# Attention with cached K and V: how K of the first units is transposed, and how the last 64 contraction rows of Q are multiplied

## The chip, the cores and the metric

The kernel runs on one core of a Trainium2 chip. The metric is the device time of one execution in microseconds (us). Before the change it is 1075.5 us, the median of three runs (1074.76 to 1076.54).

A core has TensorE (PE, matrix products into PSUM), VectorE (DVE), ScalarE (ACT), GpSimd (POOL) and SyncE (SP), which here issues every DMA. A matmul on PE has a weight load ahead of it, shown in the profile as a separate row, PEld.

## The reference, cut to what matters

Two independent problems A and B of the same shape are computed, and their outputs are joined along the last axis. Types are bf16.

```python
# B = 16, Sq = 144, D = 448, H = 16, Sk = 512, Dh = 256
q = (x @ wq).reshape(B, Sq, H, Dh).transpose(0, 2, 1, 3)
scores = einsum("bhqd,bhkd->bhqk", q, k_cache) * Dh ** -0.5
p = softmax(scores, axis=-1)
o = einsum("bhqk,bhkd->bhqd", p, v_cache)
out = o.transpose(0, 2, 1, 3).reshape(B, Sq, H * Dh) @ wo
```

## The kernel before, in words

**Units.** One batch and one head of one problem is a unit, so there are 512. Each needs Q (the product of x and 256 columns of wq), S (K times Q, scores with keys on the partitions), an exponential on ScalarE, PV (V times the exponentials), a sum over keys (a product with a matrix of ones), its reciprocal on ScalarE as exp(-ln), and a scaled evacuation into a ring of outputs on VectorE (line 1241). The output projection OP (line 1306) takes pieces of that ring in between.

**K transposed.** S needs K with the head dimension on the partitions. For units 48 and up the DMA transposes K as it loads it, 16 units (4 MB) at a time, into one of two halves of `kt_sb` (`t_load_k`, line 966). For the first 48 units (`P0`) K is loaded as it stands into slots of `v_sb` (`t_load_n`, line 987), and PE transposes it by 128x128 blocks against an identity (`t_tr`, line 1006): four blocks into a bank shared with S, which VectorE evacuates, and four into a bank shared with Q, which ScalarE evacuates (both line 1014).

**Q.** The contraction is over 448 rows, three chunks of 128 and a last one of 64. `q_pair` says how many units one Q makes: one (80 times, all of the first 48 units among them), or two units of the same head in neighbouring batches, with both batches' queries as one moving operand of 288 columns (216 times). The last 64 rows of wq stand in a tile of their own, `wr_sb`: rows for the first 128 output columns on partitions 0 to 63, and those for the other 128 on partitions 64 to 127. Two-unit Q runs the last chunk as two matmuls of 64 rows each, on the two halves of the array (line 1099). One-unit Q runs it as one full matmul of 288 columns (line 1087), against a moving tile `xz_sb` that holds x twice, each copy zero on the half that isn't its own. x is loaded transposed with rows 320 to 447 as its fourth chunk, so its last 64 rows are on partitions 64 to 127 only. VectorE copies them to partitions 0 to 63 (line 1049, for two-unit Q) or into `xz_sb` (lines 1055 and 1058), one step of the schedule ahead of the Q that reads them (`t_q_rest`).

**Order.** A Python loop over steps writes each engine's program; a recording layer (`_Sched`) adds the semaphore waits that reads and writes of the same tile or bank need. Every engine executes its program in order. One step has, on PE: half of a transposition for the unit four ahead, Q for a unit three or four ahead, S two or three ahead, the other half of the transposition, PV and the sum of the current unit, then OP pieces. SyncE's order is a list: a start table, loads by due time, and a table for the change from problem A to B. There `q0` to `q3` load B's wq in groups of four heads, each as three DMAs (lines 926, 930, 931) on one semaphore, between V loads and the K loads `k16`, `k17` and `k18`. A load that waits for a buffer holds up all that stand behind it.

**Start.** The first DMAs are K of the first two units, wq of the first four heads, then x. GpSimd meanwhile writes ones and selects the identity from them (line 917). It lies in a slot of `qt_sb` that is used for Q later.

Of the kernel before, what the change touches and what calls it, by code (L numbers as in the profile page):

```python
# [5 lines left out]
BF16 = mybir.dt.bfloat16  # L6
F32 = mybir.dt.float32
# [745 lines left out]
def bass_concat_heads__mha_block_cached__gqa_block_cached__near_ridge_kernel(  # L753
# [67 lines left out]
    with contextlib.ExitStack() as es:  # L821
# [5 lines left out]
        def ps(name, shape, dt):  # L827
            return mem.enter_context(nc.psum_tensor(name, shape, dt))

        wq_sb = sb("wq_sb", [128, 3, H * DH], BF16)  # L830
        wr_sb = sb("wr_sb", [128, H * 128], BF16)
        xz_sb = sb("xz_sb", [128, 2, 2, SQ], BF16)
        wo_sb = sb("wo_sb", [128, NWO, D], BF16)
        ring = sb("ring", [128, NWO, RC], BF16)
        kt_sb = sb("kt_sb", [128, 8, KR * 128], BF16)
# [16 lines left out]
        s_ps = [ps("s_ps%d" % i, [128, 512], F32) for i in range(3)]  # L852
        ot_ps = [ps("ot_ps%d" % i, [128, 512], F32) for i in range(2)]
        op_ps = ps("op_ps", [128, 512], F32)
        tr_ps = (s_ps[2][:, :].bitcast(BF16), qp_ps[:, 1, :].bitcast(BF16))
        ident = qt_sb[:, NQT - 1, 0, 0:128]
        id_key = (("qt", NQT - 1), -1)

        S = _Sched()
# [37 lines left out]
        def t_init():  # L897
            def e0(v):
                return v.memset(stat[:, 0:2], 0.0)
            S.add(DVE, e0, writes=[("scr", 0)], name="statz")  # L900

            def e1(a):
                a.preload_act_table_set("natural_log_exp_and_others")
                return a.activation(stat[0:1, 1:2], stat[0:1, 0:1], AF.Exp)
            S.add(ACT, e1, reads=[("scr", 0)], writes=[("scr1", 0)], name="actwarm")

            def e2(v):
                v.memset(xz_sb[64:128, :, 0, :], 0.0)
                return v.memset(xz_sb[0:64, :, 1, :], 0.0)
            S.add(DVE, e2, writes=[("xzz", 0)], name="xzz")  # L910

            def e4(g):
                return g.memset(ones[:], 1.0)
            S.add(POOL, e4, writes=[("ones", 0)], name="ones")

            def e5(g):
                return g.affine_select(ident, ones[:], pattern=[[1, 128]], compare_op=ALU.is_equal,
                                       fill=0.0, base=0, channel_multiplier=-1)
            S.add(POOL, e5, reads=[("ones", 0)], writes=[id_key], name="ident")

        def t_load_wq(pr, hg):
            cols = slice(hg * 4 * DH, (hg + 1) * 4 * DH)
            w = wqs[pr]

            def e(q):
                q.dma_start(wq_sb[:, 0:3, cols], w[0:384, cols].rearrange("(c p) n -> p c n", p=128)).then_inc(
                    sems["wq%d" % hg], 16)
                last = w[384:448, cols].rearrange("k (h e m) -> k h e m", e=2, m=128)
                dst = wr_sb[:, hg * 512:(hg + 1) * 512].rearrange("p (h m) -> p h m", m=128)
                q.dma_start(dst[0:64], last[:, :, 0, :]).then_inc(sems["wq%d" % hg], 16)  # L930
                return q.dma_start(dst[64:128], last[:, :, 1, :]).then_inc(sems["wq%d" % hg], 16)
            S.add(SP, e, writes=[(("wq", hg), pr)], dma_sem="wq%d" % hg, n_dma=3, name="wq%d.%d" % (pr, hg))

        def t_load_wo(pr, wg):
            c0 = wg * WOG
# [46 lines left out]
        def t_load_n(G):  # L982
# [4 lines left out]
                return q.dma_start(v_sb[:, sl, :, :], src).then_inc(sems["v%d" % sl], 16)  # L987
            S.add(SP, e, writes=[(("v", sl), ("n", G))], dma_sem="v%d" % sl, name="n%d" % G)

        def t_tr(U, k):  # L990
            G, j = divmod(U, UV)
            sl = v_seq["n", G] % NV
            ko = U % KR * 128

            kt_key = ("kt", U // KW % (KR // KW))
            if k == 0 and U % KW == 0:
                S.res[kt_key] = _Res()
                S.res[kt_key].version = U // KW
            bank, eng = (("s2", DVE), ("qp1", ACT))[k]
            key = (("sp", 2), "qp1")[k]  # L1000

            def e(t):
                ins = None
                for c in range(4):
                    a = (4 * k + c) * 128
                    ins = t.transpose(tr_ps[k][:, c * 128:(c + 1) * 128], v_sb[:, sl, j, a:a + 128], ident)  # L1006
                return ins
            S.add(PE, e, reads=[(("v", sl), ("n", G)), id_key], writes=[(key, ("t", U))], banks=[bank],
                  name="TR%d.%d" % (U, k))

            def ev(g):
                dst = kt_sb[:, 4 * k:4 * k + 4, ko:ko + 128]
                src = tr_ps[k][:, 0:512].rearrange("p (c q) -> p c q", c=4)
                return g.activation(dst, src, AF.Copy) if eng == ACT else g.tensor_copy(dst, src)  # L1014
            S.add(eng, ev, reads=[(key, ("t", U))], writes=[(("ktn", U % KR), U)], banks=[bank],
                  name="etr%d.%d" % (U, k))
# [25 lines left out]
            for u, sl in zip(q_units(U), free):  # L1042
                q_slot[u] = q_live[u] = sl

        def t_xr(g, n):
            gx = g % NX
            if n == 2:
                def e(v):
                    return v.tensor_copy(xt_sb[0:64, 3, gx, :], xt_sb[64:128, 3, gx, :])  # L1049
                S.add(DVE, e, reads=[(("xt", gx), g)], writes=[(("xr", gx), g)], name="xr%d" % g)  # L1050
                return
            z = g % 2

            def e0(v):
                return v.tensor_copy(xz_sb[0:64, z, 0, :], xt_sb[64:128, 3, gx, :])

            def e1(v):
                return v.tensor_copy(xz_sb[64:128, z, 1, :], xt_sb[64:128, 3, gx, :])
            for k, e in ((0, e0), (1, e1)):
                S.add(DVE, e, reads=[(("xt", gx), g), ("xzz", 0)], writes=[(("xz", z), g)], name="xz%d.%d" % (g, k))  # L1060

        xr_made = set()

        def t_q_rest(U):
            pr = unit(U)[0]
            n = q_pair(U)
            for u in q_units(U):
                g = pr * Bn + (u - pr * NU) // H
                if (g, n) not in xr_made:
                    xr_made.add((g, n))  # L1070
                    t_xr(g, n)

        def t_q(U):
            pr, b, h = unit(U)
            n = q_pair(U)
            gs = [pr * Bn + (u - pr * NU) // H for u in q_units(U)]
            xo, xe = gs[0] % NX, gs[-1] % NX
            hg = h // 4
            z = gs[0] % 2
            rest = [(("xz", z), gs[0])] if n == 1 else [(("xr", g % NX), g) for g in gs]  # L1080

            def e(t):
                ins = None
                xs_ = slice(xo, xe + 1, max(xe - xo, 1))
                wr = wr_sb[:, h * 128:(h + 1) * 128]
                if n == 1:
                    t.matmul(qp_ps[:, 0, 0:2 * SQ], lhsT=wr, rhs=xz_sb[:, z, :, :], start=True, stop=False,  # L1087
                             skip_group_check=True)
                for kc in range(3):
                    for dc in range(2):  # L1090
                        c0 = h * DH + dc * 128
                        acc = qp_ps[:, dc, 0:2 * SQ] if n == 2 else qp_ps[:, 0, dc * SQ:(dc + 1) * SQ]
                        ins = t.matmul(acc, lhsT=wq_sb[:, kc, c0:c0 + 128], rhs=xt_sb[:, kc, xs_, :],  # L1093
                                       start=(n == 2 and kc == 0), stop=(n == 1 and kc == 2),
                                       skip_group_check=(n == 1))
                if n == 2:
                    for dc in range(2):
                        p = slice(64 * dc, 64 * dc + 64)
                        ins = t.matmul(qp_ps[:, dc, 0:2 * SQ], lhsT=wr[p], rhs=xt_sb[p, 3, xs_, :],  # L1099
                                       start=False, stop=True)  # L1100
                return ins
            S.add(PE, e, reads=[(("wq", hg), pr)] + [(("xt", g % NX), g) for g in gs] + rest,
                  writes=[(bk, ("q", U)) for bk in q_banks[:n]], banks=q_banks[:n], name="Q%d" % U)

        def t_evac_q(U):
# [13 lines left out]
        def t_s(U):  # L1119
# [6 lines left out]
            for k in range(2):  # L1126
                bank = k if U < P0 else (2 * U + k) % 3

                def e(t, k=k, bank=bank):
                    ins = None  # L1130
                    for c in (2 * k, 2 * k + 1):
                        for dc in range(2):
                            ins = t.matmul(s_ps[bank][:, (c % 2) * SQ:(c % 2 + 1) * SQ],  # L1133
                                           lhsT=kt_sb[:, 2 * c + dc, ko:ko + 128],
                                           rhs=qt_sb[:, qsl, dc, :], start=(dc == 0), stop=(dc == 1))
                    return ins
                S.add(PE, e, reads=[(("qt", qsl), U), (("kt", ksl), W)] + kn, writes=[(("sp", bank), 2 * U + k)],
# [285 lines left out]
        while True:  # L1423
# [12 lines left out]
            u = i + LT  # L1436
            if 0 <= u < P0:
                t_tr(u, 0)
            for u in of_step(lq, i + 1):
                if q_pair(u):  # L1440
                    t_q_rest(u)
            for u in of_step(lq, i):
                if q_pair(u):
                    t_q_rest(u)
                    t_q(u)
                    t_evac_q(u)
            for u in of_step(ls, i):
# [138 lines left out]
```

## Time and profile before

| | |
|---|---|
| median of three runs | 1075.5 us |
| the profiled execution | 1075.5 us |
| its span, first instruction to last | 1073.7 us |
| granted TensorE clock, mean | 0.998 |
| PE, ACT, DVE, POOL busy | 98%, 74%, 70%, 59% |
| moved by DMA | 294 MB, mean 274 GB/s |
| S (L1133), PV (L1189), OP (L1306), Q (L1093, L1099) on the chain | 24, 22, 18 and 21% of the span |
| transposes (L1006) | 384 |

Matmuls are pipelined and the profile models their ends, so what a matmul costs is read from the distance between starts, and not from its duration: 128x144 matmuls are given as 226 ns long and start every 62 or 63 ns. Idle time of an engine is put down to what ended last before it resumed. The chain of work that ended last is followed back from the last instruction, at each step to what released it.

### The profile page before, as it was taken

How to read it: one execution, taken by the hardware profiler on the slowest of the kernel's cores; microseconds unless marked ns; L12 is line 12 of the kernel's file. 1: busy time of each engine (PE TensorE's matmuls, PEld its weight loads, DVE VectorE, ACT ScalarE, POOL GpSimd, SP SyncE). 2: the span in 40 equal slices, each digit the busy share in tenths (PEclk: the TensorE clock that was granted, in tenths of full speed). 3: DMA queues.
4: the chain of work that ended last, by engine and by line, in shares of the span. 5: the costliest groups of instructions: out<-in, count | busy, mean ns of one | idle time of the engine just before them, and what ended most of it. 6: DMA issues, size and time to landing. Idle time of an engine off the chain costs nothing.

```text
span 1073.7 us, 32198 instructions
## 1 busy us (share of the span) xinstructions
PE 1050.2 (98%) x12296; PEld 833.4 (78%) x12296; DVE 752.0 (70%) x2083; ACT 794.3 (74%) x2365; POOL 630.9 (59%) x1030
## 2 busy tenths in 40 slices
PE   7999999999999999999989999999999999999998
PEld 6998777777777777777867777777777777777785
DVE  4776666767766677677868676667776667777775
ACT  5876667777777777778857677777777777778785
POOL 3554555656656566666745555566665555666663
PEclk9999999999999999999999999999999999999999
DMA  9999999999999999999999999999999989999950
GB/s 340 388 325 254 311 275 299 264 249 259 259 299 289 245 252 248 286 298 272 267 296 329 265 287 305 288 304 286 305 268 277 254 241 306 274 293 233 264 192 13
DMA packets 592771, 294.13 MB, mean 274 GB/s; under 512 B 505056, under 2 KB 517856, under 8 KB 592608
## 3 DMA queue, kind: packets, MB, share of 16 engines
q1 hardware_dynamic: 592608, 291.99, 107.1%
q8 instruction: 98, 1.61, 0.6%
q14 instruction: 65, 0.53, 0.2%
HBM read 161.48 MB, written 4.13 MB: 154 GB/s over the span
## 4 chain that ended last, share of the span: by engine, by line
PE 91%; ACT 3%; DMA 3%; DVE 2%; issue 1%; SPq 0%; ACTq 0%; DVEq 0%
PE s_ps L1133 24%; PE ot_ps L1189 22%; PE op_ps L1306 18%; PE qp_ps L1093 17%; PE qp_ps L1099 4%; DMA kt_sb<-in_B_k_cache_dram 2%; ACT rinv_sb L1226 2%; PE ot_ps L1205 2%; PE qp_ps L1087 1%; ACT pt_sb L1143 1%; PE s_ps L1006 1%; PE qp_ps L1006 1%; DVE ring L1241 1%; DMA wr_sb<-in_B_wq_dram 1%; PE qp_ps L1306 1%
## 5 line engine op out<-in xcount | busy, mean ns | idle before, releaser
L1153 POOL TENSOR_TENSOR pp_sb<-pt_sb 128x288 f32<-128x288 bf16 x512 | 379.8, 742 | 347.0 <-ACT pt_sb L1143 334.1
L1143 ACT ACTIVATE pt_sb<-s_ps 128x288 bf16<-128x288 f32 x1024 | 364.6, 408 | 203.3 <-PE s_ps L1133 196.1
L1241 DVE TENSOR_TENSOR ring<-ot_ps,rinv_sb 128x288 bf16<-128x288 f32 (+2 forms) x640 | 242.0, 395 | 156.8 <-ACT rinv_sb L1226 154.5
L1133 PE MATMUL s_ps<-qt_sb,kt_sb 128*128 128x144 bf16 x4096 | 343.5, 227 | 2.5 <-DVE ring L1241 1.0
L1189 PE MATMUL ot_ps<-pt_sb,v_sb 128*128 128x144 bf16 x4096 | 340.0, 226 | 0.0
L1133 PEld LDWEIGHTS s_ps<-qt_sb,kt_sb 128*128 128x128 bf16 x4096 | 271.0, 98 | 69.9 <-DVE qt_sb L1112 3.0
L1226 ACT ACTIVATE rinv_sb<-ln_sb 64x144 f32<-64x144 f32 x928 | 298.2, 321 | 24.2
L1306 PE MATMUL op_ps<-wo_sb,ring 128*128 128x448 bf16 x1120 | 284.5, 352 | 0.0
L1189 PEld LDWEIGHTS ot_ps<-pt_sb,v_sb 128*128 128x128 bf16 x4096 | 274.2, 98 | 0.5
L1158 POOL TENSOR_TENSOR p_sb<-pp_sb 128x144 f32<-128x144 f32 x464 | 226.9, 489 | 74.8 <-DVE ps_sb L1167 10.7
L1093 PE MATMUL qp_ps<-xt_sb,wq_sb 128*128 128x288 bf16 (+1 forms) x1776 | 239.1, 271 | 5.6 <-DMA wr_sb<-in_B_wq_dram 4.1
L1093 PEld LDWEIGHTS qp_ps<-xt_sb,wq_sb 128*128 128x128 bf16 x1776 | 161.9, 98 | 71.4 <-DVE xt_sb L1049 6.1
L1256 DVE TENSOR_REDUCE run_sb<-ot_ps 128x1 bf16<-128x144 f32 x560 | 146.6, 304 | 87.5 <-ACT ln_sb L1213 55.6
L1167 DVE TENSOR_TENSOR ps_sb<-p_sb 64x144 bf16<-64x144 f32 x464 | 160.1, 345 | 37.5 <-POOL p_sb L1158 23.5
L1113 DVE CAST qt_sb<-qp_ps 128x576 bf16<-128x576 f32 x216 | 162.2, 751 | 18.1 <-PE qp_ps L1099 14.3
L1306 PEld LDWEIGHTS op_ps<-wo_sb,ring 128*128 128x128 bf16 x1120 | 93.9, 98 | 21.2
L1213 ACT ACTIVATE ln_sb<-ot_ps 128x144 f32<-128x144 f32 x232 | 67.7, 292 | 32.1 <-PE ot_ps L1205 24.4
L1099 PE MATMUL qp_ps<-xt_sb,wr_sb 64*128 64x288 bf16 x432 | 64.1, 293 | 0.0
L1205 PE MATMUL ot_ps<-ps_sb,ones 128*128 128x144 bf16 x280 | 63.3, 226 | 0.0
L1099 PEld LDWEIGHTS qp_ps<-xt_sb,wr_sb 64*128 64x128 bf16 x432 | 20.7, 93 | 51.5 <-issue 51.5
L1112 DVE CAST qt_sb<-qp_ps 128x288 bf16<-128x288 f32 x80 | 35.9, 449 | 3.0 <-PE qp_ps L1093 2.6
L1014 ACT ACTIVATE kt_sb<-qp_ps 128x512 bf16<-128x512 bf16 x48 | 29.0, 605 | 7.6 <-PE qp_ps L1006 7.6
(37 smaller groups left out, 245.9 us busy)
## 6 DMA issues: line engine op xcount, KB each, us to landing
v_sb<-in_A_v_cache_dram SPq DMA_DIRECT2D x128, 512.0 KB, 6.3
v_sb<-in_B_v_cache_dram SPq DMA_DIRECT2D x128, 512.0 KB, 6.6
v_sb<-in_A_k_cache_dram SPq DMA_DIRECT2D x24, 512.0 KB, 8.0
out_dram<-ost_sb SPq DMA_DIRECT2D x36, 112.0 KB, 5.8
wo_sb<-in_A_wo_dram SPq DMA_DIRECT2D x8, 448.0 KB, 6.7
wo_sb<-in_B_wo_dram SPq DMA_DIRECT2D x8, 448.0 KB, 8.5
wq_sb<-in_A_wq_dram SPq DMA_DIRECT2D x4, 768.0 KB, 8.0
wq_sb<-in_B_wq_dram SPq DMA_DIRECT2D x4, 768.0 KB, 8.0
```

The costliest lines, as they stand in the source:

```text
L1093: ins = t.matmul(acc, lhsT=wq_sb[:, kc, c0:c0 + 128], rhs=xt_sb[:, kc, xs_, :], start=(n == 2 and kc == 0), stop=(n == 1 and kc == 2), ski ...
L1113: return v.tensor_copy(qt_sb[:, a:b + 1:b - a, :, :], qp_ps[:, :, 0:2 * SQ].rearrange("p e (u q) -> p u e q", u=2))
L1133: ins = t.matmul(s_ps[bank][:, (c % 2) * SQ:(c % 2 + 1) * SQ], lhsT=kt_sb[:, 2 * c + dc, ko:ko + 128], rhs=qt_sb[:, qsl, dc, :], start=(dc ...
L1143: return a.activation(pt_sb[:, psl, 2 * k:2 * k + 2, :].rearrange("p b q -> p (b q)"), s_ps[bank][:, 0:2 * SQ], AF.Exp, scale=DH ** -0.5)
L1153: return g.tensor_tensor(pp_sb[:, :, :], pt_sb[:, psl, 0:2, :], pt_sb[:, psl, 2:4, :], op=ALU.add)
L1158: return g.tensor_tensor(dst, pp_sb[:, 0, :], pp_sb[:, 1, :], op=ALU.add)
L1167: return v.tensor_tensor(ps_sb[p0:p0 + 64, sl, :], p2_sb[0:64, :], p2_sb[64:128, :], op=ALU.add)
L1189: ins = t.matmul(ot_ps[ob][:, dc * SQ:(dc + 1) * SQ], lhsT=v_sb[:, vsl, j, c * DH + dc * 128:c * DH + (dc + 1) * 128], rhs=pt_sb[:, sl, c, ...
L1226: return a.activation(rinv_sb[p0:p0 + 64, sl, :], ln_sb[h0:h0 + 64, :], AF.Exp, scale=-1.0)
L1241: ins = v.tensor_tensor(ring[:, 2 * h:2 * h + 2, r0:r0 + q1 - q0], ot_ps[ob][:, 0:2 * SQ].rearrange("p (c q) -> p c q", c=2)[:, :, q0:q1], ...
L1256: return v.tensor_reduce(run_sb[:, k, j:j + 1], ot_ps[ob][:, 2 * SQ:3 * SQ], axis=AX.X, op=op)
L1306: ins = t.matmul(acc[0:m, 0:D], lhsT=ring[:, c, col0:col0 + m], rhs=wo_sb[:, c, :], start=(c == first), stop=(c == last))
```

## The change

- `t_tr` transposes K of the first 48 units as if two neighbouring bf16 were one 4-byte element: four blocks of 128 x 128 elements of 4 bytes in place of eight of 2 bytes. The identity is fp32 for that, made from a tile of fp32 ones that borrows `pp_sb`. The result has keys and the two elements of a pair side by side on a partition, so even and odd head dimensions are interleaved, and `k_nat` gives its place in `kt_sb`. The evacuations copy it as one run of 512 bf16.
- S of these units takes its weights from it with a step of two. For Q to have the same order of head dimensions, Q of these units takes its columns of wq with a step of two.
- `wr_sb`, `xz_sb` and the VectorE copies (`t_xr`, `t_q_rest`) go. wq has a fourth chunk whose partitions 0 to 63 are zeroed once, with its last 64 rows on partitions 64 to 127, so that every Q runs four full chunks of 128 rows for each half of its columns: eight matmuls of 144 columns for one unit or of 288 for two.
- A group of wq is two DMAs in place of three.

```diff
-        wq_sb = sb("wq_sb", [128, 3, H * DH], BF16)
-        wr_sb = sb("wr_sb", [128, H * 128], BF16)
-        xz_sb = sb("xz_sb", [128, 2, 2, SQ], BF16)
+        wq_sb = sb("wq_sb", [128, 4, H * DH], BF16)
...
-        tr_ps = (s_ps[2][:, :].bitcast(BF16), qp_ps[:, 1, :].bitcast(BF16))
-        ident = qt_sb[:, NQT - 1, 0, 0:128]
+        tr_ps = (s_ps[2][:, :], qp_ps[:, 1, :])
+        ident = qt_sb[:, NQT - 1, :, :].rearrange("p e q -> p (e q)").bitcast(F32)[:, 0:128]
+        ones_f = pp_sb[:, :, :].rearrange("p e q -> p (e q)")[:, 0:128]
...
-                v.memset(xz_sb[64:128, :, 0, :], 0.0)
-                return v.memset(xz_sb[0:64, :, 1, :], 0.0)
+                return v.memset(wq_sb[0:64, 3, :], 0.0)
...
+            def e6(g):
+                return g.memset(ones_f, 1.0)
...
-                last = w[384:448, cols].rearrange("k (h e m) -> k h e m", e=2, m=128)
-                dst = wr_sb[:, hg * 512:(hg + 1) * 512].rearrange("p (h m) -> p h m", m=128)
-                q.dma_start(dst[0:64], last[:, :, 0, :]).then_inc(sems["wq%d" % hg], 16)
-                return q.dma_start(dst[64:128], last[:, :, 1, :]).then_inc(sems["wq%d" % hg], 16)
+                return q.dma_start(wq_sb[64:128, 3, cols], w[384:448, cols]).then_inc(sems["wq%d" % hg], 16)
...
+        def k_nat(U):
+            c0 = U // KW % (KR // KW) * KW * 128 + U % 2 * 1024
+            return kt_sb[:, U % KW // 2, c0:c0 + 1024]
...
-                for c in range(4):
-                    a = (4 * k + c) * 128
-                    ins = t.transpose(tr_ps[k][:, c * 128:(c + 1) * 128], v_sb[:, sl, j, a:a + 128], ident)
+                for c in range(2):
+                    a = (2 * k + c) * 256
+                    ins = t.transpose(tr_ps[k][:, c * 128:(c + 1) * 128], v_sb[:, sl, j, a:a + 256].bitcast(F32), ident)
...
-                dst = kt_sb[:, 4 * k:4 * k + 4, ko:ko + 128]
-                src = tr_ps[k][:, 0:512].rearrange("p (c q) -> p c q", c=4)
+                dst = kn[:, k * 512:(k + 1) * 512]
+                src = tr_ps[k][:, 0:256].bitcast(BF16)
...
-                if n == 1:
-                    t.matmul(qp_ps[:, 0, 0:2 * SQ], lhsT=wr, rhs=xz_sb[:, z, :, :], start=True, stop=False,
-                             skip_group_check=True)
-                for kc in range(3):
-                    for dc in range(2):
-                        c0 = h * DH + dc * 128
+                for dc in range(2):
+                    for kc in range(4):
+                        c0 = h * DH
+                        cols = slice(c0 + dc, c0 + DH, 2) if U < P0 else slice(c0 + dc * 128, c0 + (dc + 1) * 128)
                         acc = qp_ps[:, dc, 0:2 * SQ] if n == 2 else qp_ps[:, 0, dc * SQ:(dc + 1) * SQ]
...
-                if n == 2:
-                    for dc in range(2):
-                        p = slice(64 * dc, 64 * dc + 64)
-                        ins = t.matmul(qp_ps[:, dc, 0:2 * SQ], lhsT=wr[p], rhs=xt_sb[p, 3, xs_, :],
-                                       start=False, stop=True)
+                        ins = t.matmul(acc, lhsT=wq_sb[:, kc, cols],
+                                       rhs=xt_sb[:, kc, xo:xe + 1:max(xe - xo, 1), :], start=(kc == 0), stop=(kc == 3))
...
+                            lhsT = (k_nat(U)[:, c * 256 + dc:(c + 1) * 256:2] if U < P0 else
+                                    kt_sb[:, 2 * c + dc, ko:ko + 128])
...
-            for u in of_step(lq, i + 1):
-                if q_pair(u):
-                    t_q_rest(u)
             for u in of_step(lq, i):
                 if q_pair(u):
-                    t_q_rest(u)
                     t_q(u)
```

## The prediction

> **What bounds the kernel now.** I read the page first (busy shares, chain), then the waits, then single units of work in the chain and in the order of time, then the loads. TensorE (PE) is busy 98% of the span, and the chain of work that ended last is 91% PE:
>
> ```profile
> PE 1050.2 (98%) x12296; PEld 833.4 (78%) x12296; DVE 752.0 (70%) x2083; ACT 794.3 (74%) x2365; POOL 630.9 (59%) x1030
> ...
> PE 91%; ACT 3%; DMA 3%; DVE 2%; issue 1%; SPq 0%; ACTq 0%; DVEq 0%
> ```
>
> So what PE is spared or given counts nearly in full, unless loads or another engine are close behind. The profiled execution took 1075.5 us, the median of the runs, and its span is 1073.7 us; I take sums against 1075.5.
>
> The chain around one two-unit Q (start, length, what, count):
>
> ```profile
> 703.43 0.73 PE qp_ps L1093 x6
> 704.16 0.23 PE qp_ps L1099 x2
> 704.39 0.61 PE s_ps L1133 x8
> 705.00 0.50 PE ot_ps L1189 x8
> ```
>
> Six full 288-column matmuls advance every 0.73/6 = 0.122 us, eight 144-column ones every 0.50/8 = 0.0625. Were the two 64-row matmuls free of side costs, they would take one 0.122 step together. But they enter the chain at 0.23, and the S group after them takes 0.61 where its twin, PV, takes 0.50. The waits say where this comes from (what waited for what: us in total, times, longest):
>
> ```profile
> PEld qp_ps L1099 <- issue: 51.5, 216, 0.5
> ...
> PEld qp_ps L1093 <- DVE xt_sb L1049: 6.1, 11, 0.8
> ...
> PE qp_ps L1093 <- DMA wr_sb<-in_B_wq_dram: 4.1, 1, 4.1
> ```
>
> The 64-row weight load stands idle 51.5/216 = 0.24 us each time with nothing to wait for: the array runs empty before the narrow pair, and again after it. The second line is Q of a new batch waiting for VectorE's copy of the last x rows; the third is the change of wq to problem B.
>
> One unit of the first stage (start, us, instruction):
>
> ```profile
> 86.02 0.39 PE L1006 MATMUL s_ps<-qt_sb,v_sb 128*128 128x128 bf16 x4
> 86.25 0.29 PE L1087 MATMUL qp_ps<-xz_sb,wr_sb 128*128 128x288 bf16 x1
> 86.37 0.54 PE L1093 MATMUL qp_ps<-xt_sb,wq_sb 128*128 128x144 bf16 x6
> ```
>
> Four transposes hold PE from 86.02 to 86.25, 0.056 us each; eight cost 0.445 per unit. Last, the loads. One K transfer is on the chain with no slack:
>
> ```profile
> 628.04 20.19 DMA kt_sb<-in_B_k_cache_dram
> 648.23 0.05 issue
> 648.28 0.68 PE s_ps L1133 x8
> ```
>
> **What the Trainium skill says.** "TensorE: Matmul & The Clock Gate", Part 3, "The mechanism": a weight load overlaps a running matmul only if its row group differs. The trace agrees for a 64-row load after a full one (0.24 us idle), but not for full loads, which share all rows and are still pulled ahead (a 98 ns load at a cadence of 62.5); there the measurement decides. Same page, "Weight-path perf modes": the fast weight load is used with 128 columns of a type other than fp32, and allows column steps; the trace has unit steps only. Same page, "LDWEIGHTS": otherwise columns/1.2 ns, an estimated 107 ns for 128; no run shows it yet. "FP8 and Floating Point Precision", "TensorE Precision Notes": true fp32 takes four passes; TensorE's "Terms" has a transpose mode that is 4 times faster for fp32, hence one pass. No trace here has either.
>
> **The change part by part.**
>
> *Two-unit Q (216 of them).* Removed: two 64-row matmuls with the emptied array; added: two full 288-column ones at the cadence of the six. Before, Q and the S after it: 0.73 + 0.23 + 0.61 = 1.57 us. After: 8 x 0.1225 + 0.50 = 1.48. Gain 0.09 each, 19.4 us for 216.
>
> *One-unit Q (80).* Before one 288 and six 144 columns (86.25 to 86.74, 0.498 us); after eight of 144, 8 x 0.0625 = 0.500. Cost 0.2 us in all.
>
> *VectorE copies.* 29 in-place copies and 14 into the zero-padded tile go. A batch's first Q waits for them, since they stand behind other VectorE work. Adding the excess over the cadence at each batch start outside the two stretches treated next: 1.06 (at 41.8), about 0.6 of the 1.16 at 114.2 (the rest is the previous Q's evacuation), 0.63 (187), 0.66 (510), 0.66 (1031) and eight of 0.25 (318 to 968): 5.6. I take 5.3, as the evacuation of the previous Q may become the next wait. Zeroing 64 rows of wq's fourth chunk is 4096 elements on 64 partitions. The present memset of 144 words takes 0.18 us; by words that scales to 14 x 0.18 = 2.6 us, done near 3.6, ahead of VectorE's first evacuation at 5.1; uncovered it would cost 1 us.
>
> *Start.* SyncE issues three DMAs for wq group 0, then x. Of the two 64 KB ones (0.74 and 0.61 us of its time) one goes. Q starts at 9.04, after x lands (8.46) and two copies. Without the copies 0.58 comes back, and x itself lands an estimated 0.4 earlier: gain 1.0. GpSimd adds one memset (0.20 in bf16) and selects in 4-byte elements (0.29 in bf16); doubled, the identity is ready by 2.3, hidden behind K's arrival at 4.36. Uncovered it would cost its 0.6.
>
> *Change of problem, 530 to 648 us.* PE stands 4.1 us until the third of the three wq DMAs lands at 540.33; the first two landed at 538.52 and 538.76. After, two DMAs, the second in 2 KB rows in place of 256 B: an estimated 538.9, gain 1.5. PE then ran at half clock for 3.4 us (granted clock 0.86 for 533 to 545), so a shorter stall may save 1.7 more. But from here loads bind: the K transfers of W18 and W19 land at 614.4 and 648.2 with 0.1 and 0.0 us to spare, and the V loads between land back to back, 1.25 us each. PE's gains up to 648 are only as large as what the DMA is spared. Between 547.14 and 552.74 two wq groups (1.8 MB) took 5.6 us; at the V rate (512 KB in 1.25 us) they would take 4.3. That is 0.65 per group, 2.6 for four. The 25 pairs in this stretch (2.3 us), its copies (0.7) and the stall all vanish in these 2.6.
>
> *Four-byte transposes (192 in place of 384).* Per unit four in place of eight, 0.445 us before. Low bound 4 x 0.056 = 0.22 (one pass, same cadence); middle 4 x 0.107 = 0.43, if the weight load without the fast path paces them; high 4 x 4 x 0.056 = 0.89. I take the middle: gain 48 x 0.017 = 0.8 us. At the low end not all of 48 x 0.22 = 10.7 is kept. ScalarE per unit has two exponentials (0.71 together), Ln 0.31, reciprocal 0.32 and evacuation 0.60, 1.94 us, and VectorE 0.42 + 0.45 + 0.53 + 0.45 = 1.85, against PE's 0.445 + 0.50 + 0.50 + 0.56 = 2.01. For the first 28 units, without output projection, PE can win only 0.07; for the 20 others 0.22: 6 us. At the high end PE loses 48 x 0.445 = 21.4. The two evacuations (415 and 605 ns) still read 512 bf16, now in one run: no change, behind PE in either case.
>
> *Strided weights (384 for Q, 384 for S).* Low bound nothing: the load is under a matmul of 62.5 ns, and at the transposes' 56 ns cadence it has to be within 56. High bound: half rate, 2 x 56 = 112 ns each, 768 x 0.049 = 37.6 us. I take nothing.
>
> *Other loads.* Early loads are tight (K of units 8 and 9 lands 0.7 us before use), but lose 0.65 us of DMA time per wq group too. I leave them at nothing; short of that, up to 1 us of the start is lost. K elsewhere lands 5 to 15 us early, so a 1.8% faster PE doesn't meet it. 16 units are 31 us: it shifts by 0.6.
>
> Sum: 191 pairs outside the loads' stretch x 0.09 = 17.2; copies 5.3; start 1.0; stretch 2.6; transposes 0.8; less 0.2. Total 26.7: 1075.5 - 26.7 = 1048.8, say 1049.
>
> **The rivals.**
>
> *The transposes run at full cadence*: 6 in place of 0.8, 1044. For it: one pass by the mode's description, a cadence set by columns. Against: no fast weight load for fp32.
>
> *The transposes take four passes*: 1049.7 + 21.4 = 1071. For it: fp32 is a four-pass type on this engine. It still ends faster.
>
> *The strided weight load paces the first stage* (slower): 1049 + 37.6 = 1087. Place: every Q and S of units 0 to 47. It decides once a strided load holds PE for 26.7/768 = 35 ns more than now, so from 97 ns. [...] Against: steps are allowed on the fast path.
>
> *Loads bind more widely*: the DMA is busy over 0.9 in nearly all slices; if PE's gain outside were halved by waits on K, 1060. Against: SyncE's own waits are for PE to free buffers, some 800 us in all.
>
> **How the numbers follow.** Middle case 0.47, full cadence 0.20, four passes 0.15, strided loads 0.14, loads 0.04. A measurement of this kernel tells 0.2% (2 us) from no change. The fast cases sum to 0.86; for mixtures (four passes with a part of the stride's cost) I move 0.03: faster 0.82, same 0.02, slower 0.16. Range: low 1041, the full-cadence case less 1.7 for the half clock and half of the stretch's 2.3; high 1072, which takes in four passes and leaves out the strided case.
>
> **What would show it.** Right: no idle weight load before a Q, Q and S together 1.48 us in steady state; no wait of a batch's first Q for VectorE; the wq stall of 4.1 us nearer 2.6; S in the first stage at 62.5 ns; transposes at 107 ns. Wrong: spacing of S and Q below unit 48 near 112 ns; transposes at 220 or more; W18 to W20 stalls that grow beyond the stretch; a new PE wait for the evacuation of Q at batch starts.

## The result, and the profile after

The changed kernel takes 1059.5 us (median of four runs, 1058.27 to 1060.47), beside 1075.65 for the kernel before in the same runs. The ratio is 0.985, with a 95% interval of 0.983 to 0.987. The forecast was 1049. Its sign is right and the time lies in the range, but 16.1 us came where 26.7 were summed up. The profiled execution took 1060.5 us, span 1058.7, so the two profiles differ by 15.0. That difference is taken apart here.

First the page of the kernel after: busy times, and the shares of the chain that ended last.

```profile
PE 1032.0 (97%) x12184; PEld 874.0 (83%) x12184; DVE 745.1 (70%) x2039; ACT 793.4 (75%) x2365; POOL 634.7 (60%) x1031
...
PE 92%; DMA 5%; ACT 1%; DVE 1%; issue 0%; SPq 0%; ACTq 0%; DVEq 0%
```

PE is busy 18.2 us less. DMA's share of the chain went from 3 to 5%: the loads on it are 51.1 us long together, before 31.2. These are not 20 us more of waiting, since a load on the chain counts with its whole length from issue to landing, and PE works during most of it. Then the chain around one two-unit Q (start, length, what, count):

```profile
691.89 1.13 PE op_ps L1270 x6
693.02 0.98 PE qp_ps L1062 x8
694.01 0.50 PE s_ps L1098 x8
694.51 0.50 PE ot_ps L1153 x8
```

Q and S take 0.98 + 0.50 = 1.48 us where they took 1.57. S, at 0.50, is no longer slower than its twin PV (before, 0.61 beside 0.50). One unit of the first stage, in order of time:

```profile
100.49 0.38 PE L1009 MATMUL s_ps<-qt_sb,v_sb 128*128 128x128 f32 x2
100.71 0.66 PE L1062 MATMUL qp_ps<-xt_sb,wq_sb 128*128 128x144 bf16 x8
101.21 0.66 PE L1098 MATMUL s_ps<-qt_sb,kt_sb 128*128 128x144 bf16 x8
101.71 0.38 PE L1009 MATMUL qp_ps<-qt_sb,v_sb 128*128 128x128 f32 x2
```

Two transposes of 4-byte elements hold PE for 0.22 us, 0.109 each, where one of bf16 took 0.056. Q and S, whose weights now go in steps of two, take 0.50 us for eight, 62.5 ns each, as before. Last, the waits, of the weight loads first (in total, times, longest):

```profile
PEld qp_ps L1062 <- issue: 11.2, 6, 7.5
```

The 51.5 us in 216 times ahead of the narrow pair are no more: of these 11.2, 7.5 are one wait, that for B's wq. And those of PE:

```profile
PE qp_ps L1062 <- DMA wq_sb<-in_B_wq_dram: 7.1, 1, 7.1
PE s_ps L1009 <- DMA v_sb<-in_A_k_cache_dram: 5.1, 2, 4.8
PE s_ps L1098 <- DMA kt_sb<-in_B_k_cache_dram: 3.6, 1, 3.6
PE qp_ps L1062 <- DMA xt_sb<-in_A_x_dram: 2.4, 1, 2.4
...
PE s_ps L1009 <- DVE run_sb L1220: 1.1, 1, 1.1
```

The waits of Q for VectorE's copies of x are gone. But the wait for B's wq grew from 4.1 to 7.1 us, and the one for the K of units 288 to 303 from 1.0 to 3.6. Before the change that wait stands under a name of VectorE:

```profile
614.51 0.66 PE L1133 MATMUL s_ps<-qt_sb,kt_sb 128*128 128x144 bf16 x8 [0.96 <-DVE ring L1241]
```

K landed at 614.37 there and PE went on 0.14 us later, as it did after the change (608.88 and 609.02), so K ended it.

**Where the gain is won and lost.** The start of PV of a unit, before less after, shows how far PE is ahead (us):

| unit | 0 | 4 | 12 | 16 | 48 | 96 | 192 | 240 | 256 | 272 | 288 | 304 | 384 | 448 | 511 |
|---|---|---|---|---|---|---|---|---|---|---|---|---|---|---|---|
| ahead | 0.96 | -0.23 | -0.67 | 0.40 | 1.25 | 4.00 | 8.41 | 10.88 | 6.94 | 7.65 | 4.00 | 5.61 | 9.63 | 12.60 | 15.06 |

Outside units 240 to 304 the change gains 15.06 + 5.27 = 20.3 us. Between those units, at the change of problem, it loses 10.88 - 5.61 = 5.27.

The chain through that stretch, in two views:

```profile
523.25 9.18 DMA wq_sb<-in_B_wq_dram
532.43 0.14 issue
532.57 2.08 PE qp_ps L1062 x8
534.64 0.96 PE s_ps L1098 x8
```

```profile
583.83 25.05 DMA kt_sb<-in_B_k_cache_dram
608.88 0.14 issue
609.02 0.66 PE s_ps L1098 x8
```

PE comes to the first Q of B 10.9 us earlier than before, but wq lands only 7.9 earlier (540.33 to 532.43). Q then takes 2.08 us and S 0.96, about twice their 0.98 and 0.50, since the clock was halved during the wait (at 528.0). The K of unit 288 lands at 608.88, before at 614.4, only 5.5 earlier. The windows of the kernel before and of the one after (stretch, its length, busy time of PE, its weight loads, DVE, ACT, POOL with counts; granted clock, DMA share, GB/s):

```profile
525.00:550.00 25.00, 20.92 (x248) 17.18 (x246) 17.00 (x43) 15.56 (x47) 13.03 (x22) 0.93 1.13 323
600.00:625.00 25.00, 24.04 (x266) 18.08 (x263) 16.70 (x46) 17.41 (x53) 14.22 (x24) 1.00 1.10 280
```

```profile
525.00:550.00 25.00, 17.95 (x186) 14.84 (x184) 12.77 (x28) 10.80 (x33) 8.51 (x14) 0.80 1.15 277
600.00:625.00 25.00, 21.43 (x221) 17.01 (x220) 13.78 (x39) 14.62 (x44) 11.76 (x19) 0.93 1.14 286
```

A mean clock of 0.80 over 25 us is 10 us at half clock; before it was 0.93, 3.4 us. SyncE's two K loads of that time, before and after (start, time that SyncE is held, what):

```profile
509.58 21.23 SPq L966 DMA_TRANSPOSE kt_sb<-in_B_k_cache_dram  x1
...
546.62 23.60 SPq L966 DMA_TRANSPOSE kt_sb<-in_B_k_cache_dram  x1
```

```profile
499.22 22.35 SPq L965 DMA_TRANSPOSE kt_sb<-in_B_k_cache_dram  x1
535.63 28.10 SPq L965 DMA_TRANSPOSE kt_sb<-in_B_k_cache_dram  x1
```

I call the time from the issue of the first of these (K of units 256 to 271) to the landing of K of units 288 to 303 the block of loads. It starts 10.4 us earlier than before, as PE does, but it takes 109.7 us in place of 104.8 for the same bytes. Of the 4.9 more, 3.4 lie between the landing of the first K and that of the last wq group: 23.3 us in place of 19.9, in which the DMA moves 299 GB/s in place of 351.

### The profile page after: what moved, and what is told of

It is laid out like the page before. It is cut to its first block, busy times and chain, and to the rows that moved or that the text cites. A ratio compares the mean times of both kernels' runs of the same rounds, so it can differ in the third digit from the quotient of the medians.

```text
span 1058.7 us, 31937 instructions
## 1 busy us (share of the span) xinstructions
PE 1032.0 (97%) x12184; PEld 874.0 (83%) x12184; DVE 745.1 (70%) x2039; ACT 793.4 (75%) x2365; POOL 634.7 (60%) x1031
## 4 chain that ended last, share of the span: by engine, by line
PE 92%; DMA 5%; ACT 1%; DVE 1%; issue 0%; SPq 0%; ACTq 0%; DVEq 0%
PE s_ps L1098 23%; PE ot_ps L1153 23%; PE qp_ps L1062 23%; PE op_ps L1270 19%; DMA kt_sb<-in_B_k_cache_dram 2%; PE ot_ps L1169 2%; DMA v_sb<-in_A_k_cache_dram 1%; PE s_ps L1009 1%; PE qp_ps L1009 1%; DMA wq_sb<-in_B_wq_dram 1%; PE qp_ps L1270 1%; ACT rinv_sb L1190 1%; DMA xt_sb<-in_A_x_dram 0%; ACT pt_sb L1107 0%; DVE qt_sb L1076 0%
## 5 line engine op out<-in xcount | busy, mean ns | idle before, releaser
L1117 POOL TENSOR_TENSOR pp_sb<-pt_sb 128x288 f32<-128x288 bf16 x512 | 383.7, 749 | 331.7 <-ACT pt_sb L1107 318.4
L1098 PEld LDWEIGHTS s_ps<-qt_sb,kt_sb 128*128 128x128 bf16 x4096 | 288.1, 98 | 57.0 <-DVE qt_sb L1076 5.2
L1062 PE MATMUL qp_ps<-xt_sb,wq_sb 128*128 128x288 bf16 (+1 forms) x2368 | 303.7, 272 | 10.0 <-DMA wq_sb<-in_B_wq_dram 7.1
L1062 PEld LDWEIGHTS qp_ps<-xt_sb,wq_sb 128*128 128x128 bf16 x2368 | 213.9, 99 | 87.6 <-issue 11.2
L1076 DVE CAST qt_sb<-qp_ps 128x576 bf16<-128x576 f32 x216 | 162.2, 751 | 25.8 <-PE qp_ps L1062 22.8
L1122 POOL TENSOR_TENSOR ps_sb<-pp_sb 128x144 bf16<-128x144 f32 x48 | 23.5, 489 | 6.9 <-PE ot_ps L1169 0.3
L1169 PEld LDWEIGHTS ot_ps<-ps_sb,ones 128*128 128x128 bf16 x280 | 27.4, 98 | 0.0
```

The source lines that it names most:

```text
L1062: ins = t.matmul(acc, lhsT=wq_sb[:, kc, cols], rhs=xt_sb[:, kc, xo:xe + 1:max(xe - xo, 1), :], start=(kc == 0), stop=(kc == 3))
L1076: return v.tensor_copy(qt_sb[:, a:b + 1:b - a, :, :], qp_ps[:, :, 0:2 * SQ].rearrange("p e (u q) -> p u e q", u=2))
L1117: return g.tensor_tensor(pp_sb[:, :, :], pt_sb[:, psl, 0:2, :], pt_sb[:, psl, 2:4, :], op=ALU.add)
L1122: return g.tensor_tensor(dst, pp_sb[:, 0, :], pp_sb[:, 1, :], op=ALU.add)
```

## The experiments

The theory after the result: the parts of the change are worth on PE about what the forecast says, and the shortfall is the loads at the change of problem. The rivals: the transposes or the strides cost something after all; the VectorE copies were worth less than thought; or the new shape of the wq load is slow.

**Q alone.** The change of Q and of its loads, with bf16 transposes and unit steps as before.

```diff
-        tr_ps = (s_ps[2][:, :], qp_ps[:, 1, :])
+        tr_ps = (s_ps[2][:, :].bitcast(BF16), qp_ps[:, 1, :].bitcast(BF16))
...
-                for c in range(2):
-                    a = (2 * k + c) * 256
-                    ins = t.transpose(tr_ps[k][:, c * 128:(c + 1) * 128], v_sb[:, sl, j, a:a + 256].bitcast(F32), ident)
+                for c in range(4):
+                    a = (4 * k + c) * 128
+                    ins = t.transpose(tr_ps[k][:, c * 128:(c + 1) * 128], v_sb[:, sl, j, a:a + 128], ident)
...
-                        cols = slice(c0 + dc, c0 + DH, 2) if U < P0 else slice(c0 + dc * 128, c0 + (dc + 1) * 128)
+                        cols = slice(c0 + dc * 128, c0 + (dc + 1) * 128)
...
```

> Q in four full chunks with two wq loads per group, as in the changed kernel, but K of the first 48 units transposed in bf16 and no steps of two. If the 4-byte transposes and the strided weights are worth nothing, as their measured steps (109 ns for each of four against 56 ns for each of eight, S and Q at 62 ns) say: within 1 us of the changed kernel's 1059.5. Rival: the first stage gained only 1.2 us by unit 48 because 4-byte transposes cost something that those steps do not show; then this run is 2 us or more below, near 1057.

Measured: 1056.0 us (1053.09 to 1056.74), ratio 0.983 (0.981 to 0.984). PE is as far ahead as with the whole change all through the first problem: 1.32 us at unit 48 and 10.80 at unit 248, beside 1.25 and 10.88. So transposes and strides together are worth nothing that can be seen up to there. Yet this kernel is 3.5 us faster, and its profile (waits of PE) shows where:

```profile
PE qp_ps L1059 <- DMA wq_sb<-in_B_wq_dram: 3.5, 1, 3.5
...
PE s_ps L1094 <- DMA kt_sb<-in_B_k_cache_dram: 2.4, 1, 2.4
```

Both waits of the change of problem are shorter, though the same loads are issued there in the same order. Its block of loads takes 103.9 us.

**B's wq and wo not loaded**, after and before the change (B is then computed with A's weights). After:

```diff
-    MID = ("k16 v127 v128 q0 v129 v130 q1 v131 q2 q3 v132 k17 v133 v134 v135 v136 v137 o0 o1 v138 o2 v139 o3 v140 o4 v141 "
-           "o5 v142 o6 o7 k18")
+    MID = "k16 v127 v128 v129 v130 v131 v132 k17 v133 v134 v135 v136 v137 v138 v139 v140 v141 v142 k18"
...
-            S.add(PE, e, reads=[(("wq", hg), pr), ("wqz", 0)] + [(("xt", g % NX), g) for g in gs],
+            S.add(PE, e, reads=[(("wq", hg), 0), ("wqz", 0)] + [(("xt", g % NX), g) for g in gs],
...
-            S.add(PE, e, reads=rd + [(("wo", wg), pr) for wg in sorted(set(c // WOG for c in cs))],
+            S.add(PE, e, reads=rd + [(("wo", wg), 0) for wg in sorted(set(c // WOG for c in cs))],
```

> The changed kernel with wq and wo of problem B never loaded (B is computed with A's weights): 7.3 MB less to load between 520 and 620 us. If what fell short of the forecast is lost to loads at the change of problem, the waits of 7.1 and 3.7 us and the half clock after them go: about 1044, and 23 to 25 us under the kernel before with the same omission. Rival: Q itself gains less than 0.09 us a time: about 1050, and 16 us under it.

> The kernel before with wq and wo of problem B never loaded (B is computed with A's weights). Its waits at the change of problem (4.1 us for wq with 1.7 us of half clock, about 1.5 us for K) go: about 1068. Read with the changed kernel under the same omission, as stated there.

Measured: after 1045.5 us (1044.98 to 1046.5), before 1068.7 (1067.66 to 1069.06). All of PE's waits of over 1 us in the changed kernel without these loads:

```profile
PE s_ps L1008 <- DMA v_sb<-in_A_k_cache_dram: 6.0, 4, 4.6
PE qp_ps L1061 <- DMA xt_sb<-in_A_x_dram: 2.4, 1, 2.4
PE s_ps L1097 <- DVE qt_sb L1075: 1.3, 5, 0.4
```

No wait on wq or on B's K is left, and the change is worth 23.2 us. In the same runs the kernel with all loads took 1074.8 before the change, so these loads cost it 6.1 us; with 1059.5 from the earlier runs they cost the changed kernel 14.0. With the loads the change was worth 16.1, so 7 to 8 us of its worth are lost to them, the larger part of the 10.6 by which it falls short of 26.7.

**The copies back.** Each batch's x is again copied by VectorE to partitions 0 to 63 (one copy a batch where the kernel before has up to two), and Q waits for it. Q multiplies what they write by zeros of wq, so this tests the copies and the wait for them, and nothing else.

```diff
...
+                def e(v, gx=gx):
+                    return v.tensor_copy(xt_sb[0:64, 3, gx, :], xt_sb[64:128, 3, gx, :])
+                S.add(DVE, e, reads=[(("xt", gx), g)], writes=[(("xr", gx), g)], name="xr%d" % g)
...
-            S.add(PE, e, reads=[(("wq", hg), pr), ("wqz", 0)] + [(("xt", g % NX), g) for g in gs],
+            S.add(PE, e, reads=[(("wq", hg), pr), ("wqz", 0)] + [(("xt", g % NX), g) for g in gs] + [(("xr", g % NX), g) for g in gs],
...
```

> The changed kernel, with VectorE's copies of the last 64 x rows back (one for each batch, in place, to partitions whose weights are zero), and Q of a batch waiting for them. If the copies' wait was worth the 5.3 us forecast: about 1064 to 1065, with PE waiting for VectorE at each change of batch. Rival: the waits are taken up elsewhere, by loads or by the evacuation of the previous Q: within 2 us of 1059.5.

Measured: 1061.9 us (1061.69 to 1062.35), 2.35 over the changed kernel, between the two. The waits of PE:

```profile
PE qp_ps L1077 <- DMA wq_sb<-in_B_wq_dram: 5.3, 1, 5.3
PE qp_ps L1077 <- DVE xt_sb L1060: 4.6, 8, 3.0
```

By units, 1.8 us are lost up to unit 248 and 1.1 from unit 304 on, while a PE that is later there waits less for wq (5.3 in place of 7.1). The cause is as forecast; its size in this form is some 2.9 us outside the change of problem, not 5.3.

**Both again, and two guesses about the loads**, in the same runs. The changed kernel and Q alone, unchanged; the changed kernel with the last 64 rows of wq in pieces of 256 bytes, as before the change; and with 120 idle matmuls ahead of the first Q of B, so that PE's clock isn't halved during the wait.

> The changed kernel beside the three runs below, on one chip. By the first comparison 1058 to 1060; if the 3.5 us between it and Q alone came from the chip, it is here nearer 1056.

> Q alone once more. PE reached unit 248 within 0.1 us of the changed kernel, so if the transposes and strides are worth nothing the two agree here within 1 us. Rival: the order or layout of the first stage's loads changes what comes later; then 2 to 4 us under the changed kernel again.

```diff
-                return q.dma_start(wq_sb[64:128, 3, cols], w[384:448, cols]).then_inc(sems["wq%d" % hg], 16)
+                last = w[384:448, cols].rearrange("k (h e m) -> k h e m", e=2, m=128)
+                dst = wq_sb[64:128, 3, cols].rearrange("k (h e m) -> k h e m", e=2, m=128)
+                q.dma_start(dst[:, :, 0, :], last[:, :, 0, :]).then_inc(sems["wq%d" % hg], 16)
+                return q.dma_start(dst[:, :, 1, :], last[:, :, 1, :]).then_inc(sems["wq%d" % hg], 16)
...
```

> The changed kernel with the last 64 rows of each wq group loaded as two DMAs in pieces of 256 bytes, as before, but into partitions 64 to 127. If the wait for wq grew because one DMA of 64 rows of 2 KB on half of the partitions lands late (2.45 us after its first part, before 0.24 and 1.8): the wait falls from 7.1 to about 5 us and the time by 2 us or more. Rival: the shape of this load doesn't matter, the queue ahead of it does: within 1 us of the changed kernel, with the wait where it was.

```diff
+                for _ in range(120):
+                    ins = t.matmul(qp_ps[:, 0, 0:128], lhsT=ones[:, :], rhs=ones[:, :], start=True, stop=True)
...
```

> The changed kernel with 120 matmuls of 128 columns without use ahead of the first Q of problem B (6.7 us of PE at its full clock, inside the wait for wq). If the half clock after that wait costs 2 to 3 us: 2 to 3 us under the changed kernel, with full clock after the wait. Rival: PE that goes faster there only waits longer for K of unit 288: within 1 us.

Measured: the changed kernel again 1059.7 us (1057.76 to 1061.98), Q alone again 1056.6 (1055.44 to 1059.67). The difference of 3.2 is there again, though the ranges overlap. In small pieces 1060.1 (1059.26 to 1061.08), with a wq wait of 6.1 us beside 6.4 in the changed kernel again: the shape of that load is not the cause. With idle matmuls 1059.5 (1058.2 to 1060.53). There the window of 525 to 550 us has a clock of 1.00, and PE is some 1 us further ahead at unit 256 (9.68 beside 8.73). But the wait on K shows (waits of PE):

```profile
PE s_ps L1108 <- DMA kt_sb<-in_B_k_cache_dram: 4.0, 1, 4.0
```

What PE won it waits for again 60 us later, and the median is 0.2 us from that of the changed kernel again. In the stretch the loads set the time, and the halved clock is a companion of the wait, not a loss of its own.

**wq's first group ahead of K**, so that its wait can't arise:

```diff
-    MID = ("k16 v127 v128 q0 v129 v130 q1 v131 q2 q3 v132 k17 v133 v134 v135 v136 v137 o0 o1 v138 o2 v139 o3 v140 o4 v141 "
+    MID = ("q0 k16 v127 v128 v129 v130 q1 v131 q2 q3 v132 k17 v133 v134 v135 v136 v137 o0 o1 v138 o2 v139 o3 v140 o4 v141 "
...
-            if (fn, args) == mid[0]:
+            if (fn, args) == mid[1]:
```

> The changed kernel with the first group of B's wq issued ahead of the K transfer k16 in place of behind it. If only the order of these loads makes PE wait (7.1 us for wq): that wait goes, and the time falls by 5 us or more, to about 1054. If the queue is full from here to K of unit 304 and only its total counts: PE stands instead for K of unit 256, which now comes 6 us later, and the time is within 2 us of the changed kernel.

Measured: 1056.4 us (1055.08 to 1057.62), ratio 0.982 (0.981 to 0.984): some 3 under the changed kernel. Waits of PE:

```profile
PE ot_ps L1153 <- DMA v_sb<-in_B_v_cache_dram: 3.0, 1, 3.0
PE s_ps L1098 <- DMA kt_sb<-in_B_k_cache_dram: 2.9, 1, 2.9
...
PE qp_ps L1062 <- DMA wq_sb<-in_B_wq_dram: 2.0, 1, 2.0
```

The 7.1 us for the first group are gone. V, K and the second wq group now ask for 7.9, where wq and K together asked for 10.7 (7.1 and 3.6).

**OP pieces kept for the wait.** The matmuls of the output projection that fall due in units 242 to 250 are held back, so that PE has work when it comes to wq; with the changed kernel, and with Q alone. By the trace they are 18, not the 16 that were expected.

```diff
-                while fifo[bank] and fifo[bank][0][2] <= i and credit >= 1 and (bank == "qp" or i >= op_hold):
+                while (fifo[bank] and fifo[bank][0][2] <= i and credit >= 1 and (bank == "qp" or i >= op_hold)
+                       and not NU - 14 <= i < NU - 5):
```

> The changed kernel with 16 output projection matmuls of problem A (3.0 us of PE) kept back from units 243 to 250 and run just ahead of the first Q of B, where PE waits for wq. If the loads set the time here, work moved into the wait is free, but PE reaches K's buffers earlier and the loads can't follow: 0 to 3 us under the changed kernel. Rival: the wait grows by what was moved, within 1 us.

> Q alone with the same 16 matmuls kept back: 0 to 3 us under Q alone, near 1055, which would be the fastest of these kernels.

Measured: 1058.9 us (1057.23 to 1062.11) and 1057.2 (1055.21 to 1061.25). The wq waits fell to 4.7 and 2.0, the waits on K were 4.0 and 2.4, and neither time moved by more than about 1 us. This edit could hardly win anything: the matmuls that were moved had been done ahead of the wait anyway, so when wq lands PE has done no more than before. At unit 256 it is 7.05 us ahead beside 6.94 without the edit, and with Q alone 9.90 beside 11.5.

**Both of the better ones together**: Q alone with wq's first group ahead of K.

> Q in four chunks with bf16 transposes (as in Q alone), and wq group 0 of the second problem issued ahead of the transposing load of K of units 256 to 271 (as in the run with that order). Nothing is left out. Each of the two alone stood some 3.4 us under the changed kernel (1056.0 to 1056.6, and 1056.35). If the two act on different costs, they add: 1053 (1052 to 1054), with no wait for wq group 0 and waits on V, wq group 1 and K of under 5 us together. If both are the same thing, the loads of the change of problem done sooner, they do not add: 1055.5 to 1056.5, with waits on V, wq group 1 and K of 5 to 8 us together. I hold the second to be likelier, 6 in 10.

Measured: 1061.4 us (1059.88 to 1062.24), ratio 0.987 (0.986 to 0.989). Neither expectation holds; the new order loses 5 us on Q alone. Its waits:

```profile
PE qp_ps L1059 <- DMA wq_sb<-in_B_wq_dram: 4.7, 1, 4.7
PE s_ps L1094 <- DMA kt_sb<-in_B_k_cache_dram: 4.6, 1, 4.6
```

A part of the cause can be read from SyncE's queue. First this kernel, then the changed kernel with the same order:

```profile
498.76 0.37 SPq L974 DMA_DIRECT2D v_sb<-in_A_v_cache_dram  x1
504.61 0.37 SPq L924 DMA_DIRECT2D wq_sb<-in_B_wq_dram  x1
505.02 0.51 SPq L926 DMA_DIRECT2D wq_sb<-in_B_wq_dram  x1
505.58 20.35 SPq L961 DMA_TRANSPOSE kt_sb<-in_B_k_cache_dram  x1
```

```profile
504.36 0.51 SPq L930 DMA_DIRECT2D wq_sb<-in_B_wq_dram  x1
504.92 18.38 SPq L965 DMA_TRANSPOSE kt_sb<-in_B_k_cache_dram  x1
```

In the first of the two, SyncE stands from 499.1 to 504.6 until PE has read A's first wq group for the last time, so K goes out 6.4 us later than in Q alone; in the second it goes out 5.7 us later than in the changed kernel. It then takes less time: in the changed kernel with this order K lands 3.2 us later than without it (526.9 and 523.7), in Q alone 4.6 us later (528.0 and 523.3). That difference of 1.4 is a small part only. At the K of unit 288 the order has won 5.3 us in the one and lost 5.1 in the other, and what makes the rest isn't shown. So the gain of the run with the order alone isn't shown to be the order's.

**All profiles in one table.** The block of loads in the profiled execution of each kernel that loads B's weights. Where wq's first group goes ahead of K, the block has that group less to load:

| kernel | K of 256 issued | block takes | K of 288 lands | profiled time |
|---|---|---|---|---|
| before | 509.6 | 104.8 | 614.4 | 1075.5 |
| after | 499.2 | 109.7 | 608.9 | 1060.5 |
| after again | 499.1 | 108.7 | 607.8 | 1060.9 |
| small pieces | 499.4 | 108.3 | 607.7 | 1059.3 |
| OP pieces kept | 499.3 | 110.4 | 609.7 | 1062.1 |
| copies back | 501.0 | 107.4 | 608.4 | 1062.0 |
| idle matmuls | 499.7 | 106.8 | 606.6 | 1059.4 |
| wq's first group ahead of K | 504.9 | 98.7 | 603.6 | 1057.6 |
| Q alone | 499.2 | 103.9 | 603.1 | 1053.1 |
| Q alone again | 499.5 | 104.0 | 603.5 | 1055.8 |
| Q alone, OP pieces kept | 499.5 | 105.0 | 604.6 | 1055.2 |
| Q alone, wq's first group ahead | 505.6 | 102.6 | 608.2 | 1059.9 |

With the new Q, the time less the landing of that K is 450 to 454 us in all of them (before 461: there Q is slower behind it too). Where that K lands by 604.6 the profiled time is 1053 to 1058 us, where it lands from 606.6 on it is 1059 to 1062. So the end follows the landing of K of unit 288, and the kernels differ mainly in how long the block takes.

## Why the prediction was right and wrong

**Right on PE's own work.** Two-unit Q with S went from 1.57 to 1.48 us. From unit 48 to 240 PE gains 9.63, where 94 pairs make 94 x 0.09 = 8.5; with the copies back it gains 8.53 there, so the rest is copies. The 4-byte transposes take 109 ns, the middle value of 107 (an estimate from "TensorE: Matmul & The Clock Gate", section "LDWEIGHTS", of the Trainium skill, for loading 128 columns of weights), so four cost 0.436 where eight cost 0.445, and both rivals about them fall. The strided weights cost nothing; the adverse rival decided from 97 ns, and 62.5 were measured. One-unit Q is 0.50 as said. That transposes and strides are together worth nothing visible on PE is shown by Q alone; the cost of each alone is read from starts.

**Wrong on the stretch of the change of problem: the step that failed.** The forecast let the loads shift with PE and spared the DMA 2.6 us there, 0.65 per wq group for rows of 2 KB in place of 256 bytes: two groups that had taken 5.6 us (547.14 to 552.74) were to take 4.3. The same two took 6.2, from the V load ahead of them that landed at 540.74 to 546.99, and 6.2 with Q alone (536.04 to 542.28). Nothing was spared, and PE, 10.9 us ahead, lost 5.3. The forecast also read that K of unit 288 had landed with 0.1 us to spare before the change, where PE had stood 1.0 us for it. With the 2.6 that were to be won this is 7.9 of the 11.6 us by which the profiled gain (15.1 at the last unit) falls short of 26.7. Both runs without B's weights show it: without these loads the change is worth 23.2 us, with them 15 to 16. The loads did shift, by 10.4 us at the issue of K of unit 256, but the block behind it took 4.9 longer. The shape of the rows has no part in it (1060.1 with 256 bytes).

The forecast had also left room for a shorter stall with less time at half clock. The stall grew, and the clock followed it. The Trainium skill (same page, section "What's actually happening") has the clock halved after an idle window of about 3.4 us, and the windows run freely. The lengths in the trace agree: 10.2 us at half clock from 528.0 and 3.4 from 609.9, three such windows and one. But PE had stood for only 2.5 us (from 525.5) when the clock fell, and with Q alone again it fell after a wait of 2.9, so here a window need not be idle throughout. The idle matmuls show that the clock isn't what sets the time.

That the time lies in the range is in part luck: the range's upper part was meant for transposes in four passes, and what came in its place was the loads.

The rival that loads bind more widely named 1060, which is near the time, but not its mechanism: no wait for a transposing load of K came in outside this stretch.

**Wrong on the start, by about 2 us.** Of the 3.4 forecast up to unit 48 (1.0 for the start, 1.66 for two batch starts, 0.8 for the transposes, less the one-unit Q) 1.25 came. x was issued 0.8 us earlier (2.45, before 3.26) but landed later (9.00, before 8.46), so Q started at 9.14, before at 9.04. What the earlier clock gave at unit 0 (0.96, which varies between runs) was gone at unit 4: PE stood 1.1 us from 22.7 on (put to line 1220 in the waits, but to the load of K with Q alone again). K of units 8 and 9 landed 0.1 us before PE went on, at 23.6, and before the change at 22.8. All twelve kernels with the new Q are between 0.3 us behind and 1.3 ahead at unit 0, and all stand 0.1 to 0.8 behind at unit 4: the loads of the first K set the time there. Here too wq came no cheaper: the second, third and fourth group of A landed 2.6, 4.1 and 2.9 us after the load ahead of them, before 2.6, 2.6 and 2.7. The forecast had named the tight loads, counted on wq's smaller cost for them, and put the loss at nothing.

**The copies: right mechanism, size off.** They were priced at 5.3; put back in, they cost 2.9 in the profile outside the change of problem, and 2.35 in the medians. This form has one copy where the kernel before has up to two, so it bounds their worth from below.

**What stays open.** In three pairs of runs the block of loads takes 4.8 to 5.8 us longer with the whole change than with Q alone, although the loads are issued in the same order and PE is nearly as far on at unit 248. SyncE is held longer by the same K loads (22.4 and 28.1 beside 20.4 and 25.9 us), and this repeats (22.1 and 27.8 beside 20.0 and 25.8). The hold is hardly the cause: in all traces SyncE is let go 1.9 to 4.6 us before such a load lands, so it lasts about as long as the transfer, and with wq in small pieces it was 23.9 in place of 27.8 while that K landed at 564.7 beside 564.9.

One difference can be seen in the traces. A load raises its semaphore in 16 steps, as its parts land. For the three V loads between the wq groups the last part comes 1.5 to 2.2 us after the other 15 with the whole change (1.0 to 1.3 when run again), and 0.1 to 0.3 with Q alone, in both runs. Before the change it is 1.2 to 1.4, where the block was short, so this isn't the whole of it. What makes one part late, no run here tells. Nor is it known why the bytes between K's landing and the last wq group flow more slowly than before the change. Of the kernels run in which nothing is left out, Q alone and the changed kernel with wq's first group ahead of K are fastest, near 1056 us, some 3 under the changed kernel.

## What to carry to other kernels

Where PE is sped up next to a stretch whose loads already end late, count its gain up to that stretch as lost in part: compare how much earlier the stretch's loads are issued with how much earlier its last one lands. A wait filled or removed inside such a stretch can come back in large part at its next loads (here 7.9 us of 10.7), so look for the last load and for what holds the queue ahead of it. Don't price a load by the size of its rows alone: 0.65 us per group was expected here from larger rows, and none came. A pair of narrow matmuls ahead of which the weight load stands idle (0.24 us each time here) can cost more than the zeros of two full ones: here 0.09 us a pair.

## What was not expected of the hardware

- A load with transposition of the same 4 MB of K holds SyncE between 16.1 and 28.1 us within one execution, and nearly the same for a given place in the program when the changed kernel is run again (within 0.8 us for the first 27 of the 29 loads), less so when Q alone is (up to 2.1).
- Weights with a step of two columns of bf16 are loaded under a cadence of 62.5 ns without any loss.
- A transposition with 4-byte elements takes 109 ns for 128x128 where bf16 takes 56, and in the first 12 us of the kernel 214 where bf16 takes 107: per byte it is no faster.
- The clock can be halved after a wait of less than 3 us (2.9 with Q alone again), and until PE's last units it stays halved for one, two or three times 3.41 us in these traces.
